# The first block's attention by pairs of heads instead of by tiles of tokens, in a fused attention and two-layer expert kernel

## The chip, the core and the metric

The kernel runs on one core of one Trainium2 chip. The metric is the device time of one launch in microseconds (us). The core has five engines with an instruction queue each: TensorE (PE, matmuls and transposes into PSUM), VectorE (DVE), ScalarE (ACT), GpSimd (POOL) and SyncE (SP, which issues the loads). They run independently and wait for each other by semaphores; each works through its own queue in order.

## What is computed

Linear attention with a normalisation, then a dense feed-forward layer with squared ReLU, then a feed-forward layer of 8 experts of which each token uses one. All inputs are float32.

```python
kv = np.einsum('bhsd,bhse->bhde', k, v)            # batch 4, heads 8, 576 tokens, head width 64
out = np.einsum('bhsd,bhde->bhse', q, kv)
rms = np.sqrt(np.mean(out * out, axis=-1, keepdims=True) + 1e-06)
x = out / rms * g_norm                             # then reshaped to 2304 tokens x 512
h = x @ w_in                                       # 512 -> 2048
x = np.maximum(h, 0.0) ** 2 @ w_out                # 2048 -> 512
logits = x @ w_gate                                # 8 experts; the largest one takes the token
y = gate * (np.maximum(x @ w1[e], 0.0) @ w2[e])    # e: the token's expert, within its capacity
```

## The kernel before

The 2304 tokens are 18 tiles of 128, in 6 blocks of TB = 3 tiles (BT = 384 tokens); a batch has 576 tokens, so block 0 lies inside batch 0. The 8 heads are 4 pairs of 128 columns.

**Attention of a block.** `kv(b, p)` multiplies k and v of pair p of batch b over five chunks into one PSUM bank (line 209) and copies the two 64 x 64 diagonal pieces into `kvb` (lines 211 and 212, ACT and DVE). `attn_out(t)` multiplies tile t of q with all four pairs of `kvb` (line 227), squares the result (line 235, ACT), sums the squares of each head (line 237, DVE) and takes mean and inverse root by a power (lines 239 and 241, POOL). `attn_mul(t)` scales the rows (line 245, DVE). `attn_tr(t)` transposes the four 128-column pieces (line 254, PE) and writes them as two float32r parts: the rounded value times `g_norm` (line 258, ACT) and the remainder (line 259, DVE). `xT[j]` of a block then holds [part, pair, token].

**First feed-forward layer.** Its hidden width 2048 is cut into NF = 16 slices f. A unit (j, f) is block j with slice f: `mm1` has 12 matmuls, three passes over each of the four 128-row chunks of `xT` (chunk c is pair c of the heads), then ReLU, square and split (lines 273 to 285), and `mm2`, two units later, adds its product to the block's output (line 292). Block 0 runs alone for LEAD = 4 units and then alternates with block 1. The tasks of block 1's attention are dealt out over units 0 to 3 by a plan.

**Weights of that layer.** They come in as 64-bit words (`load_m`, line 148). `cvt_m(f)` rebuilds float32 from the words: ACT scales the high halves of both matrices (line 167), DVE shifts and joins (lines 168, 169 and 173, on 1024 columns where both matrices go together). `split_m(f)` makes the float32r pair: a cast (line 182, ACT) and the remainder (line 183, POOL).

**Order.** `tc.manual_schedule(engines={SP})` (line 529) keeps the order of the code on SP's queue alone; on the other engines a scheduler orders the instructions. The loads come in the order pair 0 of k and v, two constants, pairs 1 to 3, the three q tiles, then words of f = 0 and f = 1, then the second batch's k and v with the words of f = 2 among them.

```python
        for p in range(NPAIR):
            kv(0, p)
        for t in range(TB):
            attn_out(t)
        for t in range(TB):
            attn_mul(t)
            attn_tr(t)
        for f in range(2):
            cvt_m(f)
            split_m(f, wpool)
```

Of the kernel before, what the change touches and what calls it, by code (L numbers as in the profile page):

```python
# [7 lines left out]
F32 = mybir.dt.float32  # L8
# [18 lines left out]
def attn_moe_kernel(ctx: ExitStack, tc: tile.TileContext, cap, kp, vp, qt, gn, wm, wg, wgt, w1, w2, ident, tri, out):  # L27
# [83 lines left out]
    def after_scatters(dma):  # L111
        dma = getattr(dma, "ins", dma)
        for i in scattered["disp"]:
# [27 lines left out]
    def load_m(f):  # L141
        for i in range(2):
            if f < 12:
                s = wpool.tile([P, 512], I64, tag="w", name="st64")
            else:
                s = stage.tile([P, 512], I64, tag="st", name="st64")
            stg["m", f, i] = s
            nc.sync.dma_start(out=s, in_=wm[f, :, i])

    def cvt_m(f):  # L150


        ws = [stg.pop(("m", f, i)).bitcast(I32).rearrange("p (n t) -> p n t", t=2) for i in range(2)]
        if f < 12:
            h = wpool2.tile([P, 2, 512], F32, tag="w", name="ch")
            o = wpool2.tile([P, 2, 512], F32, tag="w", name="cf")
            parts = [(h, o, slice(0, 2))]
# [6 lines left out]
        for h, o, sl in parts:  # L164
            hi, oi = h.bitcast(I32), o.bitcast(I32)
            for n, w in enumerate(ws[sl]):
                nc.scalar.activation(out=h[:, n, :], in_=w[:, :, 1].bitcast(F32), func=AF.Copy, scale=2.0 ** -112)
            nc.vector.tensor_scalar(oi, hi, -(1 << 31), None, op0=ALU.bitwise_and)
            nc.vector.scalar_tensor_tensor(
                out=oi, in0=hi, scalar=3, in1=oi, op0=ALU.logical_shift_left, op1=ALU.bitwise_or  # L170
            )
            for n, w in enumerate(ws[sl]):
                nc.vector.scalar_tensor_tensor(
                    out=oi[:, n, :], in0=w[:, :, 0], scalar=29, in1=oi[:, n, :],
                    op0=ALU.logical_shift_right, op1=ALU.bitwise_or,
                )

    def split_m(f, pool):
        os = cvt.pop(f)
        for o, d in zip(os, (wi, wo)):  # L180
            w = d[f] = pool.tile([P, 2, 512], F32R, tag="w", name="w")
            nc.scalar.copy(w[:, 0, :], o)  # L182
# [22 lines left out]
    def kv(b, p):  # L205
        k, v = kt.pop((b, p)), vt.pop((b, p))
        ps = misc()
        for c in range(NCH):
            nc.tensor.matmul(ps[:, :P], lhsT=k[:, c, :], rhs=v[:, c, :], start=c == 0, stop=c == NCH - 1)
# [52 lines left out]
        )  # L262


    gt = {}

    def mm1(s):
# [2 lines left out]
        n = 0  # L270
        for c in range(KD):
            for a, m in PASSES:
                nc.tensor.matmul(  # L273
                    h, lhsT=wi[f][:, a, c * P:(c + 1) * P], rhs=xT[j][:, m, c, :],
                    start=n == 0, stop=n == 3 * KD - 1,
                )
                n += 1


        r = gpool.tile([P, BT], F32, tag="rr", name="rr", bufs=2)  # L280
# [245 lines left out]
    MIDDLE = 416  # L526
    units = []

    with tc.manual_schedule(engines={mybir.EngineType.SP}):

        cold = gpool.tile([P, BT], F32, tag="rr", name="cold", bufs=2)[:, :P]
        nc.vector.memset(cold, 0.0)
# [10 lines left out]
        nc.vector.tensor_copy(ecap, ecap_i)  # L543
        nc.vector.tensor_copy(base, ecap_i)

        for p in range(NPAIR):
            load_kv(0, p)
            if p == 0:
                nc.sync.dma_start(out=id_sb, in_=ident)
                nc.sync.dma_start(out=gn_sb, in_=gn)  # L550
        for t in range(TB):
            load_q(t)
        load_m(0)
        load_m(1)
        load_kv(1, 0)
        load_kv(1, 1)
# [119 lines left out]
        for s in range(len(units)):  # L676
# [388 lines left out]
```

## Time and profile before

| what | value |
|---|---|
| median of 3 runs | 759.33 us (758.04 to 760.86) |
| the profiled execution's own time | 763.88 us |
| its span, first to last instruction | 762.10 us |
| busy: PE, DVE, ACT, POOL | 715.9, 370.7, 310.2, 292.1 us |
| mean granted clock of PE | 0.985 of full |
| 8.69 to 31.16 us: PE busy, DVE busy | 16.03, 13.63 of 22.47 us |
| 31.16 to 75.45 us: PE busy, DVE busy | 36.84, 40.41 of 44.29 us |
| 75.45 to 155 us: PE busy, DVE busy | 79.55, 51.00 of 79.55 us |

Times in the trace count from the first instruction of the span. A busy time is the union of an engine's instructions. Matmuls of float32 show as two records each (so the five matmuls of one `kv` are ten records), those of float32r as one. [...] "Idle before" an instruction is the time in which its engine had nothing to run, with the engine and line whose result ended it. DMA share 1.0 means that the core's 16 DMA engines were all moving data.

### The profile page before, as it was taken

Reading aid. Unit: us, or ns where it says so; the run is one execution under the profiler, and the core shown is the slowest. Engines: PE = TensorE matmul, PEld = TensorE weight load, DVE = VectorE, ACT = ScalarE, POOL = GpSimd, SP = SyncE. Lnnn points to the kernel's source line nnn. Section 1 sums busy time; section 2 is a strip of 40 time slices with the busy share of each in tenths; the row PEclk is TensorE's granted clock in tenths of the full one; section 3 lists DMA queues with packets and bytes.
Section 4 is the critical chain, followed back from the end, with each engine's and each line's share of the span. In section 5 each row is a group of like instructions: output and inputs, shape, how many; then the busy total and the mean of one; then the engine's idle time right before and its main releaser. Section 6 shows DMA issues by size and latency. Waiting matters only on the chain. (4 is left out here: it accounts for less than half of the span.)

```text
span 762.1 us, 11995 instructions
## 1 busy us (share of the span) xinstructions
PE 715.9 (94%) x3988; PEld 639.7 (84%) x3988; DVE 370.7 (49%) x829; ACT 310.2 (41%) x650; POOL 292.1 (38%) x288
## 2 busy tenths in 40 slices
PE   6688999999999999999999999999998999999874
PEld 6677999998999999889898988897887997898663
DVE  2989767448963593349445953331123220332011
ACT  2455455233222322232233354344367452665352
POOL 1576243112022200220220286224488637596570
PEclk9899999999999999999999999999999999999979
DMA  8946898311032202200100365152456536356520
GB/s 326 372 166 208 270 359 304 117 25 55 9 114 76 66 18 69 82 16 1 55 15 1 129 208 176 35 173 92 148 172 232 189 117 200 119 190 203 185 73 10
DMA packets 38020, 102.42 MB, mean 134 GB/s; under 512 B 4451, under 2 KB 4707, under 8 KB 37920
## 3 DMA queue, kind: packets, MB, share of 16 engines
q1 hardware_dynamic: 34912, 91.99, 36.0%
q0 software_dynamic: 3008, 9.10, 3.2%
q8 instruction: 63, 1.03, 0.6%
q14 instruction: 37, 0.30, 0.1%
HBM read 77.78 MB, written 23.91 MB: 133 GB/s over the span
## 5 line engine op out<-in xcount | busy, mean ns | idle before, releaser
L273 PE MATMUL pk<-xT,w 128*128 128x384 f32 x1152 | 223.1, 341 | 7.2 <-POOL w L183 4.6
L292 PE MATMUL pk<-w,g 128*128 128x512 f32 x864 | 218.4, 394 | 2.5 <-ACT g L284 2.5
L273 PEld LDWEIGHTS pk<-xT,w 128*128 128x128 f32 x1152 | 201.5, 188 | 17.0 <-POOL w L183 5.8
L194 POOL TENSOR_TENSOR w<-st,w 128x512 fp32r<-128x512 f32 x128 | 161.7, 1300 | 88.2 <-ACT w L190 86.6
L292 PEld LDWEIGHTS pk<-w,g 128*128 128x128 f32 x864 | 160.2, 188 | 31.7 <-ACT g L284 3.1
L281 ACT ACTIVATE rr<-pk 128x384 f32<-128x384 f32 x96 | 47.1, 492 | 153.3 <-PE pk L273 153.1
L810 PE MATMUL hb<-x,w 128*128 128x256 f32 (+2 forms) x672 | 95.3, 301 | 2.5 <-issue 1.7
L810 PEld LDWEIGHTS hb<-x,w 128*128 128x128 f32 x672 | 92.8, 188 | 4.2 <-issue 2.1
L864 DVE SCALAR_TENSOR_TENSOR g<-hb,g 128x576 fp32r<-128x576 f32 (+3 forms) x72 | 40.7, 585 | 106.2 <-ACT g L863 106.1
L283 DVE TENSOR_TENSOR pk<-pk,rr 128x384 f32<-128x384 f32 x96 | 54.0, 563 | 74.4 <-ACT rr L281 73.6
L102 POOL DMA_INDIRECT disp<-y,sli x18 | 19.1, 1059 | 173.1 <-DVE sli L409 52.9
L354 DVE SCALAR_TENSOR_TENSOR junk<-y,wgb 128x512 f32<-128x512 f32 x120 | 78.0, 684 | 0.7 <-ACT y L312 0.6
L190 ACT CAST w<-st 128x512 fp32r<-128x512 f32 x128 | 71.5, 620 | 11.6 <-DMA st<-in_w 11.1
L284 ACT CAST g<-pk 128x384 fp32r<-128x384 f32 x96 | 46.0, 480 | 72.4 <-DVE pk L283 70.6
L285 DVE TENSOR_TENSOR g<-pk,g 128x384 fp32r<-128x384 f32 x96 | 53.3, 556 | 36.6 <-ACT g L284 35.9
L183 POOL TENSOR_TENSOR w<-cf,w 128x512 fp32r<-128x512 f32 x32 | 46.8, 1482 | 61.4 <-ACT w L182 56.9
L896 PE MATMUL hb<-w,g 128*128 128x512 f32 x264 | 64.1, 399 | 2.9 <-DVE g L864 2.6
L896 PEld LDWEIGHTS hb<-w,g 128*128 128x128 f32 x264 | 48.9, 188 | 14.8 <-DVE g L864 3.2
L863 ACT ACTIVATE g<-hb 128x576 fp32r (+3 forms) x72 | 35.2, 513 | 33.7 <-PE hb L810 31.9
L102 POOL DMA_INDIRECT out<-o,meta x22 | 21.3, 970 | 46.8 <-ACT o L904 18.4
L912 DVE SCALAR_TENSOR_TENSOR o<-bk,meta,o 64x512 f32<-64x512 f32 x3 | 2.3, 753 | 69.1 <-ACT o L911 50.6
L239 POOL TENSOR_SCALAR ms<-ss 128x8 f32<-128x8 f32 x18 | 4.6, 255 | 77.0 <-DVE ss L237 76.7
(134 smaller groups left out, 651.1 us busy)
## 6 DMA issues: line engine op xcount, KB each, us to landing
st<-in_w SPq DMA_DIRECT2D x64, 512.0 KB
st<-in_wm SPq DMA_DIRECT2D x32, 512.0 KB
disp<-zrow SPq DMA_DIRECT2D x9, 1028.0 KB
xr<-disp SPq DMA_DIRECT2D x32, 257.0 KB
k<-in_kp SPq DMA_DIRECT2D x16, 320.0 KB
v<-in_vp SPq DMA_DIRECT2D x16, 320.0 KB
q<-in_qt SPq DMA_DIRECT2D x18, 256.0 KB
out<-zrow SPq DMA_DIRECT2D x9, 512.0 KB
```

The costliest lines, as they stand in the source:

```text
L183: nc.gpsimd.tensor_tensor(w[:, 1, :], o, f32(w[:, 0, :]), op=ALU.subtract)
L190: nc.scalar.copy(w[:, 0, :], s[:, i, :])
L194: e.tensor_tensor(w[:, 1, :], s[:, i, :], f32(w[:, 0, :]), op=ALU.subtract)
L273: nc.tensor.matmul(h, lhsT=wi[f][:, a, c * P:(c + 1) * P], rhs=xT[j][:, m, c, :], start=n == 0, stop=n == 3 * KD - 1,)
L281: nc.scalar.activation(out=r, in_=h, func=AF.Relu)
L283: nc.vector.tensor_tensor(h, h, r, op=ALU.mult)
L284: nc.scalar.copy(g[:, 0, :], h)
L285: nc.vector.tensor_tensor(g[:, 1, :], h, f32(g[:, 0, :]), op=ALU.subtract)
L292: nc.tensor.matmul(ysets[j == 1][i], lhsT=g[:, a, i * P:(i + 1) * P], rhs=wo[f][:, m, :], start=f == 0 and n == 0, stop=f == NF - 1 and n ...
L354: nc.vector.scalar_tensor_tensor(out=junk, in0=yt[j * TB + i][:, :DM], scalar=1.0, in1=wgb[e // 2][:, e % 2, :], op0=ALU.mult, op1=ALU.mul ...
L810: nc.tensor.matmul(h, lhsT=w1_at(e, f // 2, a, c)[:, f % 2 * P:(f % 2 + 1) * P], rhs=x[:, m, c, o:o + w], start=k == 0, stop=k == 3 * KD - 1,)
L896: nc.tensor.matmul(ps[:k, :], lhsT=lhs(f, a), rhs=we2[e, f][:, b, :], start=n == 0, stop=n == len(passes) * NF2 - 1,)
```

## The change

It rewrites the start of the program, up to the weights of f = 1, and leaves the rest as it is.

- **Loads**: after pair 0 of k and v and the two constants come the three q tiles, then pairs 1 and 2, the first matrix's words of f = 0, pair 3, the second matrix's words of f = 0, and from there on the old order.
- **Attention of block 0**: three new functions work on one pair of heads and all three tiles at a time. `first_out(p)` multiplies each q tile with pair p into 384 columns of one bank and does the squares, sums and power on six head-and-tile columns; `first_mul(p)` scales; `first_tr(p)` transposes three pieces and writes chunk p of `xT[0]`. So four operations of 384 columns stand where three of 512 stood. The PSUM banks go round over six (`pk[2:8]`) instead of three.
- **Words of f = 0**: rebuilt one matrix at a time on 512 columns, the first between the sums of pair 2 and the scaling of pair 1, the second between pair 2's transposes and the scaling of pair 3.
- **Order**: `tc.manual_schedule()` now holds the written order on all engines up to there. After it, `in_order` adds edges for the scheduler alone (no semaphore): ACT's scalings for f = 1 come after the last transposed chunk (`marks["first"]`), those for f = 2 after the casts of f = 1 (`marks["split"]`), and the matmuls of the second batch's `kv` in units 0 to 3 after unit 0's last matmul (`marks["kv"]`).

```diff
-        for p in range(NPAIR):
-            load_kv(0, p)
-            if p == 0:
-                nc.sync.dma_start(out=id_sb, in_=ident)
-                nc.sync.dma_start(out=gn_sb, in_=gn)
+        load_kv(0, 0)
+        nc.sync.dma_start(out=id_sb, in_=ident)
+        nc.sync.dma_start(out=gn_sb, in_=gn)
         for t in range(TB):
             load_q(t)
-        load_m(0)
+        load_kv(0, 1)
+        load_kv(0, 2)
+        load_m(0, (0,))
+        load_kv(0, 3)
+        load_m(0, (1,))
         load_m(1)
...
-        for p in range(NPAIR):
-            kv(0, p)
+        free[:] = pk[2:8]
+        kv(0, 0)
+        first_out(0)
+        kv(0, 1)
+        first_out(1)
+        first_mul(0)
+        first_tr(0)
+        kv(0, 2)
+        first_out(2)
+        c_in, c_out = cvt_m(0)
+        c_in()
+        first_mul(1)
+        first_tr(1)
+        split_m(0, wpool, (0,))
+        kv(0, 3)
+        first_out(3)
+        first_mul(2)
+        first_tr(2)
+        c_out()
+        first_mul(3)
+        first_tr(3)
+        split_m(0, wpool, (1,))
         for t in range(TB):
-            attn_out(t)
-        for t in range(TB):
-            attn_mul(t)
-            attn_tr(t)
-        for f in range(2):
-            cvt_m(f)
-            split_m(f, wpool)
+            qtt.pop(t)
+        free[:] = ysets[1]
+
+    with tc.manual_schedule(engines={mybir.EngineType.SP}):
+        marks["cvt"] = marks["first"]
+        for c in cvt_m(1):
+            c()
+        split_m(1, wpool)
+        marks["cvt"] = marks["split"]
```

The new functions:

```python
    def first_out(p):
        ps = ops[p] = misc()
        for t in range(TB):
            nc.tensor.matmul(
                ps[:, t * P:(t + 1) * P], lhsT=qtt[t][:, p, :], rhs=kvb[0][:, p, :],
                start=t == 0, stop=t == TB - 1, skip_group_check=True,
            )
        x = xst[p] = ypool.tile([P, ROW], F32, tag="y", name="x")[:, :BT] if p < 3 else apool.tile(
            [P, DM], F32, tag="x", name="x")[:, :BT]
        nc.scalar.activation(out=x, in_=ps[:, :BT], func=AF.Square)
        ss = small.tile([P, 2 * TB], F32, tag="ss", name="ss")
        nc.vector.tensor_reduce(out=ss, in_=x.rearrange("p (h e) -> p h e", e=DH), axis=AX.X, op=ALU.add)
...

    def first_mul(p):
        r, ps = rst.pop(p), ops.pop(p)
        nc.vector.tensor_tensor(
            xst[p].rearrange("p (h e) -> p h e", e=DH), ps[:, :BT].rearrange("p (h e) -> p h e", e=DH),
            r.rearrange("p (h o) -> p h o", o=1).to_broadcast([P, 2 * TB, DH]), op=ALU.mult,
        )

    def first_tr(p):
        x = xst.pop(p)
        ps = misc()
        for t in range(TB):
            nc.tensor.transpose(ps[:, t * P:(t + 1) * P], x[:, t * P:(t + 1) * P], id_sb)
        d = xt_tile(0)
        marks["first"] = nc.scalar.activation(out=d[:, 0, p, :], in_=ps[:, :BT], func=AF.Copy, scale=gn_sb)
        nc.vector.scalar_tensor_tensor(
            out=d[:, 1, p, :], in0=ps[:, :BT], scalar=gn_sb, in1=f32(d[:, 0, p, :]), op0=ALU.mult, op1=ALU.subtract,
        )
```

The order on PE, from the first `kv` on (`k`, `v`, `q`: loaded tiles; `kvb`: the products of pairs; `id_sb`: transposes; `pk`: PSUM banks; `xT,w`: `mm1`). Before:

```order
L209 MATMUL pk_92<-v,k 128x128 x5
L209 MATMUL pk_93<-v,k 128x128 x5
L209 MATMUL pk_94<-v,k 128x128 x5
L209 MATMUL pk_92<-v,k 128x128 x5
L227 MATMUL pk_93<-kvb_127,q 128x128 x4
L227 MATMUL pk_94<-kvb_127,q 128x128 x4
L227 MATMUL pk_92<-kvb_127,q 128x128 x4
L254 MATMUL pk_93<-id_sb,x 128x128 x4
L254 MATMUL pk_94<-id_sb,x 128x128 x4
L254 MATMUL pk_92<-id_sb,x 128x128 x4
L209 MATMUL pk_93<-v,k 128x128 x5
```

After, from the second pair on:

```order
L223 MATMUL pk_91<-v,k 128x128 x5
L285 MATMUL pk_92<-kvb_127,q 128x128 x3
L310 MATMUL pk_93<-id_sb,x 128x128 x3
L223 MATMUL pk_94<-v,k 128x128 x5
L285 MATMUL pk_89<-kvb_127,q 128x128 x3
L310 MATMUL pk_90<-id_sb,x 128x128 x3
L223 MATMUL pk_91<-v,k 128x128 x5
L326 MATMUL pk_87<-xT,w 128x384
L285 MATMUL pk_92<-kvb_127,q 128x128 x3
L326 MATMUL pk_87<-xT,w 128x384 x5
L310 MATMUL pk_93<-id_sb,x 128x128 x3
L326 MATMUL pk_87<-xT,w 128x384 x3
```

The four `kv` and three outputs that followed each other directly are now separated by the transposes of the pair before, and unit 0's matmuls stand among them; the second batch's `kv` (last row of the first piece) has moved behind unit 0.

The order on DVE over the same place (`ss`: sums of squares; `cf`, `ch`: rebuilt words; `st`: loaded words). Before, from the first sum on:

```order
L237 TENSOR_REDUCE ss<-x 128x8 x2
L245 TENSOR_TENSOR x<-pk_93,r 128x512
L237 TENSOR_REDUCE ss<-x 128x8
L245 TENSOR_TENSOR x<-pk_94,r 128x512
L168 TENSOR_SCALAR cf<-ch 128x1024
L259 SCALAR_TENSOR_TENSOR xT<-pk_93,gn_sb,xT 128x4x128
L259 SCALAR_TENSOR_TENSOR xT<-pk_94,gn_sb,xT 128x4x128
L245 TENSOR_TENSOR x<-pk_92,r 128x512
L169 SCALAR_TENSOR_TENSOR cf<-ch,cf 128x1024
L168 TENSOR_SCALAR cf<-ch 128x1024
```

After, from pair 2 on:

```order
L228 COPY kvb_127<-pk_94 64x64
L293 TENSOR_REDUCE ss<-x 128x6
L182 TENSOR_SCALAR cf<-ch 128x512
L183 SCALAR_TENSOR_TENSOR cf<-ch,cf 128x512
L187 SCALAR_TENSOR_TENSOR cf<-st_171,cf 128x512
L301 TENSOR_TENSOR x<-pk_92,r 128x384
L313 SCALAR_TENSOR_TENSOR xT<-pk_90,gn_sb,xT 128x384
L228 COPY kvb_127<-pk_91 64x64
L293 TENSOR_REDUCE ss<-x 128x6
L301 TENSOR_TENSOR x<-pk_89,r 128x384
L313 SCALAR_TENSOR_TENSOR xT<-pk_93,gn_sb,xT 128x384
```

The three operations on f = 0's first words stand ahead of the scaling of pair 1, and the words of f = 1, which before stood among the tiles, come only after the last chunk.

## Rows read from the trace of the kernel before

**Rows 1.** The page, first part: busy time, share of the span, instructions.
```profile
span 762.1 us, 11995 instructions
PE 715.9 (94%) x3988; PEld 639.7 (84%) x3988; DVE 370.7 (49%) x829; ACT 310.2 (41%) x650; POOL 292.1 (38%) x288
```

**Rows 2.** Busy time by stretch; the first line names the columns.
```profile
core 0: us, PE busy (x) PEld busy (x) DVE busy (x) ACT busy (x) POOL busy (x), PEclk, DMA share, GB/s
8.69:31.16 22.47, 16.03 (x103) 15.21 (x103) 13.63 (x23) 8.92 (x20) 6.53 (x9) 0.78 1.04 399
31.16:75.45 44.29, 36.84 (x199) 31.59 (x199) 40.41 (x51) 25.60 (x49) 32.21 (x22) 1.00 0.61 209
75.45:155.00 79.55, 79.55 (x400) 72.04 (x399) 51.00 (x79) 35.22 (x70) 22.32 (x19) 1.00 0.74 254
```

**Rows 3.** The same view, cut where the granted clock changes; columns as above.
```profile
8.30:11.70 3.40, 2.98 (x14) 3.01 (x15) 0.23 (x1) 0.21 (x1) 0.00 (x0) 0.50 1.03 405
11.70:21.90 10.20, 6.11 (x50) 5.42 (x49) 4.80 (x9) 4.17 (x9) 5.29 (x8) 1.00 1.04 407
21.90:28.70 6.80, 4.77 (x23) 4.80 (x24) 6.27 (x9) 2.50 (x5) 1.24 (x2) 0.50 1.04 384
```

**Rows 4.** PE's timeline, 0 to 37 us: start, length, what, [idle before, releaser].
```profile
4.96 1.28 PE L209 MATMUL pk<-v,k 128*128 128x128 f32 x10
8.72 5.00 PE L209 MATMUL pk<-v,k 128*128 128x128 f32 x30 [2.48 <-DMA v<-in_vp]
13.55 3.00 PE L227 MATMUL pk<-kvb,q 128*128 128x128 f32 x24
19.04 0.63 PE L254 MATMUL pk<-id_sb,x 128*128 128x128 f32 x4 [2.49 <-DVE x L245]
...
32.62 2.38 PE L273 MATMUL pk<-xT,w 128*128 128x384 f32 x12 [0.62 <-POOL w L183]
36.53 0.80 PE L273 MATMUL pk<-xT,w 128*128 128x384 f32 x3 [1.53 <-POOL w L183]
```

**Rows 5.** The timeline of all engines, DVE's rows, 18 to 31 us.
```profile
18.20 0.69 DVE L245 TENSOR_TENSOR x<-pk,r 128x512 f32<-128x512 f32 x1 [1.19 <-POOL r L241]
25.77 0.75 DVE L259 SCALAR_TENSOR_TENSOR xT<-pk,gn_sb,xT 128x512 fp32r<-128x512 f32 x1 [0.25 <-ACT xT L258]
29.15 1.29 DVE L173 SCALAR_TENSOR_TENSOR cf<-st,cf 128x512 int32<-128x512 int32 x2
```

**Rows 6.** Groups by line, 8 to 31.16 us: xcount | busy us, mean ns | idle before.
```profile
L169 DVE SCALAR_TENSOR_TENSOR cf<-ch,cf 128x1024 int32<-128x1024 int32 x2 | 2.4, 1218 | 0.0
L173 DVE SCALAR_TENSOR_TENSOR cf<-st,cf 128x512 int32<-128x512 int32 x4 | 2.6, 686 | 0.0
L245 DVE TENSOR_TENSOR x<-pk,r 128x512 f32<-128x512 f32 x3 | 2.1, 688 | 1.9 <-POOL r L241 1.9
L212 DVE COPY kvb<-pk 64x64 f32<-64x64 f32 x5 | 1.1, 228 | 6.5 <-ACT kvb L211 6.4
L254 PE MATMUL pk<-id_sb,x 128*128 128x128 f32 x12 | 2.3, 329 | 6.1 <-DVE x L245 6.1
L241 POOL TENSOR_TENSOR r<-ms,expo 128x8 f32<-128x8 f32 x3 | 5.2, 1739 | 0.2
L167 ACT ACTIVATE ch<-st 128x512 f32<-128x512 f32 x6 | 3.7, 664 | 0.0
L211 ACT COPY kvb<-pk 64x64 f32<-64x64 f32 x6 | 1.2, 204 | 10.0 <-PE pk L209 10.0
```

**Rows 7.** Groups by line, 75.45 to 155 us: the units' 384-column and the 512-column operations.
```profile
L283 DVE TENSOR_TENSOR pk<-pk,rr 128x384 f32<-128x384 f32 x20 | 11.3, 563 | 20.1 <-ACT rr L281 20.1
L168 DVE TENSOR_SCALAR cf<-ch 128x512 int32<-128x512 int32 x8 | 3.7, 468 | 0.0
L281 ACT ACTIVATE rr<-pk 128x384 f32<-128x384 f32 x20 | 9.8, 492 | 25.5 <-PE pk L273 25.4
```

**Rows 8.** Groups by line, 31.16 to 75.45 us: POOL's remainders and ACT's casts.
```profile
L183 POOL TENSOR_TENSOR w<-cf,w 128x512 fp32r<-128x512 f32 x16 | 25.4, 1612 | 19.3 <-ACT w L182 19.2
L182 ACT CAST w<-cf 128x512 fp32r<-128x512 f32 x15 | 8.9, 621 | 3.9 <-DVE cf L173 3.8
```

More of the change, by code (lines that the diff above doesn't have):

```diff
@@ L117, in after_scatters, with in_order @@
             )
+    def in_order(later, first):
+        later, first = getattr(later, "ins", later), getattr(first, "ins", first)
+        tc.add_manual_dep(
+            later, first.name, mybir.DependencyInfo(mybir.DependencyClass.NoSync, mybir.DependencyReason.SCHED_ONLY),
+            reason="the order in which the loads come in",
+        )
+    marks = {}
     kt, vt, qtt = {}, {}, {}
@@ L139, in load_w, with load_m @@
         nc.sync.dma_start(out=stg[key], in_=src)
-    def load_m(f):
-        for i in range(2):
+    def load_m(f, which=(0, 1)):
+        for i in which:
             if f < 12:
@@ L156, in cvt_m @@
             o = wpool2.tile([P, 2, 512], F32, tag="w", name="cf")
-            parts = [(h, o, slice(0, 2))]
+            parts = [(h[:, a:a + n], o[:, a:a + n], slice(a, a + n)) for a, n in (((0, 1), (1, 1)) if f == 0 else ((0, 2),))]
             cvt[f] = [o[:, i, :] for i in range(2)]
@@ L163, in cvt_m, with cvt_part, split_m @@
             cvt[f] = [o[:, 0, :] for o in os]
[L164 to L168, printed above, removed]
+        return [lambda part=part: cvt_part(ws, *part) for part in parts]
+    def cvt_part(ws, h, o, sl):
+        hi, oi = h.bitcast(I32), o.bitcast(I32)
+        for n, w in enumerate(ws[sl]):
+            a = nc.scalar.activation(out=h[:, n, :], in_=w[:, :, 1].bitcast(F32), func=AF.Copy, scale=2.0 ** -112)
+            if "cvt" in marks:
+                in_order(a, marks["cvt"])
+        nc.vector.tensor_scalar(oi, hi, -(1 << 31), None, op0=ALU.bitwise_and)
+        nc.vector.scalar_tensor_tensor(
+            out=oi, in0=hi, scalar=3, in1=oi, op0=ALU.logical_shift_left, op1=ALU.bitwise_or
+        )
+        for n, w in enumerate(ws[sl]):
             nc.vector.scalar_tensor_tensor(
-                out=oi, in0=hi, scalar=3, in1=oi, op0=ALU.logical_shift_left, op1=ALU.bitwise_or
-            )
[L172 to L182, printed above, removed]
+                out=oi[:, n, :], in0=w[:, :, 0], scalar=29, in1=oi[:, n, :],
+                op0=ALU.logical_shift_right, op1=ALU.bitwise_or,
+            )
+    def split_m(f, pool, which=(0, 1)):
+        for i in which:
+            o = cvt[f][i]
+            w = (wi, wo)[i][f] = pool.tile([P, 2, 512], F32R, tag="w", name="w")
+            marks["split"] = nc.scalar.copy(w[:, 0, :], o)
             nc.gpsimd.tensor_tensor(w[:, 1, :], o, f32(w[:, 0, :]), op=ALU.subtract)
@@ L208, in kv @@
         for c in range(NCH):
-            nc.tensor.matmul(ps[:, :P], lhsT=k[:, c, :], rhs=v[:, c, :], start=c == 0, stop=c == NCH - 1)
+            a = nc.tensor.matmul(ps[:, :P], lhsT=k[:, c, :], rhs=v[:, c, :], start=c == 0, stop=c == NCH - 1)
+            if "kv" in marks:
+                in_order(a, marks["kv"])
         d = kvb[b % 2]
@@ L272, in mm1 @@
             for a, m in PASSES:
-                nc.tensor.matmul(
+                a = nc.tensor.matmul(
                     h, lhsT=wi[f][:, a, c * P:(c + 1) * P], rhs=xT[j][:, m, c, :],
@@ L277, in mm1 @@
                 n += 1
+        if s == 0:
+            marks["kv"] = a
         r = gpool.tile([P, BT], F32, tag="rr", name="rr", bufs=2)
@@ L527, in attn_moe_kernel @@
     units = []
-    with tc.manual_schedule(engines={mybir.EngineType.SP}):
+    with tc.manual_schedule():
         cold = gpool.tile([P, BT], F32, tag="rr", name="cold", bufs=2)[:, :P]
@@ L683, in attn_moe_kernel @@
             if j == 0 and f + 2 < NF:
-                cvt_m(f + 2)
+                for c in cvt_m(f + 2):
+                    c()
+                marks.pop("cvt", None)
                 split_m(f + 2, wpool if f + 2 < 12 else wpool2)
@@ L694, in attn_moe_kernel @@
                 p_()
+            if s == LEAD:
+                marks.pop("kv", None)
             fl = s - at[NB - 1, 0]
```

13 lines of the change are left out of this document (added).

## The prediction

> **What bounds the kernel now.** The page's first part comes first [rows 1]: TensorE (PE) is busy 94% of a span of 762.10 us. The share of busy time in three stretches says where the rest is [rows 2]: from 75.45 us to 155 PE is busy without a gap, and in the two stretches before that it isn't. So a change that touches only the start is worth what it does to the moment at which that dense stretch begins, and the order of instructions shows that nothing after the first dozen feed-forward units moves. I therefore keep a ledger for PE from 8.69 us, where the second pair's matmuls begin, to the dense stretch: its matmuls are the same before and after, so the stretch begins later by whatever is added in idle time and in time lost at half clock.
>
> Before, the ledger reads: idle 22.47 - 16.03 = 6.44 us and then 44.29 - 36.84 = 7.45 us [rows 2]. [...] Sum 17.8 us.
>
> PE's timeline says what the idle time waits for [rows 4]: the second pair of k and v until 8.72 us, then the transposes for the normalised rows (6.1 us, released by VectorE (DVE) [rows 6]), then POOL's remainders of the weights for units 0 and 1. In the second stretch DVE is busy 40.41 of 44.29 us [rows 2]: it rebuilds weight words there. By 30.44 us (29.15 + 1.29) DVE has rebuilt the words of f = 0 and f = 1, and the last attention row leaves it at 26.52 us (25.77 + 0.75) [rows 5].
>
> **The change, part by part.** *Loads.* Three q loads (3 x 256 KB) go ahead of pairs 1 to 3. At 399 GB/s with the DMA engines full [rows 2] that is 1.9 us, so the second pair's matmuls start at 8.7 + 1.9 = 10.6 us. The q are then there by 9.0 us (640 KB earlier), so pair 0's output matmuls (0.75 us) run in that gap. The weight words fall between the pairs; bytes and number of loads are the same, f = 0's first half arrives near 13.5 us and is wanted near 19, so that part costs nothing.
>
> *A round.* PE now runs kv(p+1), output(p+1), transposes(p), and DVE reduce(p+1), multiply(p), remainder(p); each step waits for the one before on another engine. Durations: kv 1.28 (10 records); copies 0.20 on ScalarE (ACT) and 0.23 on DVE; output 12 matmuls in 3.00, so 0.75 for 3; transposes 0.63 for four, so 0.5 for three [rows 4, 6]. Operations of 384 columns do not stand there for attention; the nearest rows are the units' own, 0.49 on ACT and 0.56 on DVE [rows 7]; bounds are three quarters of the 512-column row (0.69, so 0.52) and that row itself [rows 6]. With 0.15 us from DVE to PE (18.20 + 0.69 to 19.04) and 0.03 elsewhere:
> 1.28 + 0.20 + 0.23 + 0.75 + 0.49 + 0.56 + 0.56 + 0.50 + about 0.5 of handovers = 5.1 us.
>
> Three such rounds make 15.2 us. POOL's power (1.74 [rows 6]) lies beside the next pair's steps. Before, the four kv ran back to back and the three tiles overlapped; now PE waits in every round.
>
> *Half of f = 0's words in the second round, half after the third.* DVE's three operations on 512 columns take 0.47 + 0.69 + 0.69 = 1.85 us [rows 6, 7], and they stand ahead of multiply(1) and multiply(3) in DVE's order, so both lie on the path: 1.95 us in round two; in the tail ACT 0.55 (transposed, between 0.49 and 0.69), 0.66 (words), DVE 1.85, multiply 0.56, transposes 0.65, ACT 0.55, DVE 0.56 and handovers, 5.5 us. The last remainder thus leaves DVE at 10.6 + 15.2 + 1.95 + 5.5 = 33.25 us, against 26.52: 6.7 us later at full clock. Unit 0, interleaved, ends 0.5 us behind it, near 33.8, against 34.6 before (ten matmuls from 32.62): that is what the change wins.
>
> *f = 1 and f = 2.* Their ACT scalings must now follow the last transposed chunk and f = 1's splits. After ACT's cast (0.62) and two scalings (1.33), DVE needs 0.69 + 1.22 + 1.29 and 1.13 for unit 0: f = 1 ends near 39.0 instead of 30.44, its first remainder near 41.2 (0.62 + 1.61 [rows 8]), and unit 1's third matmul, which began at 36.53 [rows 4], goes there. Behind it on PE wait unit 1, then attention tiles 3 to 5 and the next units. The 15 matmuls of three of the second block's kv pairs, now ordered behind unit 0, cost nothing: they fill PE's wait from 33.8 on.
>
> *Extra work.* Four operations where three stood: 4 x 0.56 - 3 x 0.69 = 0.17 us for each of reduce, multiply and remainder, 0.5 us of DVE in all, already in the walk. POOL's extra power (1.74) and the small operation ahead of it cost nothing: POOL is busy 6.53 of 22.47 us in that stretch [rows 2, 6].
>
> [...] In [rows 2] DVE is busy 13.63 of 22.47 us in the first stretch, while PE waits 6.1 us for it. [...]
>
> *Sum.* PE's work between 8.69 and 33.8 us: 0.75 + 3 x 1.28 + 3 x 0.75 + 4 x 0.5 + 2.38 (unit 0's twelve [rows 4]) = 11.2 us, idle 25.1 - 11.2 = 13.9. For the rest I take the idle time of before, 7.45 less the 0.62 inside unit 0 [rows 4], 6.8 us: DVE and POOL have the same list there. It could be 3.9 less, DVE's whole idle time in that stretch, or 2 more, since f = 1 and f = 2 now come one after the other. At full clock: 13.9 + 6.8 - 17.8 = +2.9 us. Half clock: before, it followed PE's gap of 6.24 to 8.72, then 16.55 to 21.9, where PE ran 1.26 us. The first gap stays, so most of kv(1) runs at half (0.9 lost); if the path's PE steps (3.84 + 2.25 + 2.0 and 0.4 of unit 0, 8.5 us) get it for the same share as before (7.75 of 16.03), 4.1 is lost. I take the middle, 2.5. Sum **+5.4 us**: 759.33 + 5.4 = **764.7**. The ledger is that of the profiled execution, which took 763.88 us (span 762.10), 4.55 above the median; a profiled one after the change would be near 763.88 + 5.4 = 769.3. The 384-column steps at their bounds move the walk by -0.4 to +1.3 us (some ten of them on the path).
>
> **Rivals.** *Overlap wins (not slower).* If the spread-out matmuls keep the clock at full (0 lost) and DVE has no idle time behind 33.8: 2.9 - 3.9 = -1.0, 758.3; if besides the rounds hide the weight words (1.95 + 1.85 = 3.8 us), -4.8, 754.5. For it: DVE is only 61% busy in the first stretch. Against: in DVE's order the words stand ahead of multiply. It decides if the last remainder leaves DVE before about 29 us. [...]
> *DVE's backlog absorbs it.* If DVE closes up its 3.88 us of idle time [rows 2] and the clock costs 0.9: 2.9 + 0.9 - 3.9 = -0.1, 759.2. For: DVE is the busiest there; against: its waits are chains through POOL and PE that stay.
> *Half clock throughout.* PE idles 13.9 of 25.1 us in the new walk against 6.44 of 22.47; were the clock at half for all of the path, 8.5 instead of 2.5: 2.9 + 8.5 = +11.4, 770.7 at most; with half of the added 6.0 hidden, +8.4, 767.7. For: both earlier drops followed sparse stretches; against: PE's gap from 16.55 to 19.04 us did not end the full clock until 21.9 [rows 3, 4]. [...]
>
> **Chances.** Forecast (+3 to +8) 0.55, half clock throughout 0.15, absorbed 0.2, overlap wins 0.1. About 0.5%, 3.8 us, is what a measurement here can tell from no change. Four fifths of the first case and the second lie beyond it (0.44 + 0.15, less 0.01 for the walk's own error): slower 0.58; faster than 755.5 only with the words hidden too, 0.07; same 0.35. The range takes the absorbed end with the clock's lower bound and reaches to the half-clock case: 759.0 to 768.5.
>
> **What would show it.** Right: second kv near 10.6 us; transposes at intervals of 5 us or more; the last remainder (a 384-column write of xT on DVE) near 33 us or later; unit 0 done near 34 and unit 1's third matmul past 40; dense stretch later by 3 to 8 us. Wrong: that remainder before 29 us, or unit 1 before 37. If those times come late and the dense stretch isn't later, the idle time behind 33.8 us was mis-sized.

## The result, and the profile after

The changed kernel takes 770.89 us (median of 4, 770.39 to 771.19), the kernel before 760.1 (758.04 to 764.13): ratio 1.0136, interval 1.0108 to 1.0164. It is 10.8 us slower where the forecast had 5.4 more, and outside the range. The direction was forecast, and so were both mechanisms, waits in every round and half clock; the size of the second wasn't.

The profiled execution took 770.39 us. The page's first part [rows 1 before]:

```profile
span 768.6 us, 12006 instructions
PE 724.1 (94%) x3988; PEld 644.7 (84%) x3988; DVE 368.1 (48%) x834; ACT 310.3 (40%) x652; POOL 290.3 (38%) x290
```

PE does the same 3988 matmuls in 8.2 us more busy time, so the clock is the first suspect. PEclk is the share of full speed that the profile shows as granted to PE; "full clock" is a PEclk of 1.00, "half clock" one of 0.50. Busy time by stretch, cut where it changes; the last row is the same 31 us that are used below to compare kernels:

```profile
core 0: us, PE busy (x) PEld busy (x) DVE busy (x) ACT busy (x) POOL busy (x), PEclk, DMA share, GB/s
10.50:31.00 20.50, 13.76 (x58) 12.18 (x57) 5.95 (x12) 4.25 (x10) 6.92 (x9) 0.50 0.99 377
31.00:34.40 3.40, 1.90 (x9) 1.09 (x8) 2.02 (x4) 1.19 (x3) 1.52 (x2) 1.00 0.57 186
34.40:41.20 6.80, 4.68 (x17) 3.40 (x17) 4.11 (x8) 2.71 (x5) 1.27 (x1) 0.50 0.21 78
41.20:68.50 27.30, 22.57 (x134) 18.78 (x133) 21.20 (x33) 15.10 (x31) 15.67 (x13) 1.00 0.51 174
68.50:71.90 3.40, 2.86 (x11) 2.69 (x12) 1.61 (x3) 0.69 (x1) 2.17 (x2) 0.50 0.00 0
8.69:40.00 31.31, 19.54 (x76) 15.77 (x76) 11.43 (x22) 8.42 (x18) 10.12 (x13) 0.58 0.82 307
```

The same 31 us of the kernel before:

```profile
8.69:40.00 31.31, 22.72 (x141) 21.38 (x142) 21.36 (x31) 13.98 (x30) 15.34 (x15) 0.84 0.99 380
```

Against [rows 3]: half clock for 20.5 us at a stretch, through the first three of the attention's four pairs, then twice more, with PE busy 13.76 + 4.68 + 2.86 = 21.3 us instead of 7.75. DVE, which was busy 21.36 of these 31.31 us, is now busy 11.43.

PE's timeline [rows 4 before], the serial rounds and unit 1:

```profile
10.20 2.25 PE L223 MATMUL pk<-v,k 128*128 128x128 f32 x10 [1.40 <-DMA v<-in_vp]
13.01 1.65 PE L285 MATMUL pk<-kvb,q 128*128 128x128 f32 x6 [0.56 <-DVE kvb L228]
16.41 0.90 PE L310 MATMUL pk<-id_sb,x 128*128 128x128 f32 x3 [1.76 <-DVE x L301]
17.11 2.34 PE L223 MATMUL pk<-v,k 128*128 128x128 f32 x10
...
25.29 0.90 PE L310 MATMUL pk<-id_sb,x 128*128 128x128 f32 x3 [3.63 <-DVE x L301]
...
38.02 1.66 PE L326 MATMUL pk<-xT,w 128*128 128x384 f32 x3 [0.67 <-ACT xT L312]
...
46.01 1.32 PE L326 MATMUL pk<-xT,w 128*128 128x384 f32 x6 [0.23 <-POOL w L197]
```

The reader should see both things at once: each round waits in series as forecast (kv, output, transposes, each behind another engine), and each PE step in it is far longer than at full clock: kv 2.34 us where 1.28 stood, output 1.65 (0.75 was expected, and it took 0.94 with the clock at 1.00, as shown below). On DVE [rows 5 before], the reductions of pairs 1 to 3, the last remainder and the end of f = 1's words:

```profile
15.21 0.55 DVE L293 TENSOR_REDUCE ss<-x 128x6 f32<-128x384 f32 x1 [2.26 <-ACT x L291]
22.21 0.55 DVE L293 TENSOR_REDUCE ss<-x 128x6 f32<-128x384 f32 x1 [2.26 <-ACT x L291]
31.09 0.55 DVE L293 TENSOR_REDUCE ss<-x 128x6 f32<-128x384 f32 x1 [2.26 <-ACT x L291]
38.00 0.62 DVE L313 SCALAR_TENSOR_TENSOR xT<-pk,gn_sb,xT 128x384 fp32r<-128x384 f32 x1 [1.61 <-ACT xT L312]
42.72 1.28 DVE L187 SCALAR_TENSOR_TENSOR cf<-st,cf 128x512 int32<-128x512 int32 x2
```

Rounds of 7.0 and 8.9 us, the last remainder done at 38.6.

**The gauge.** Unit 24 lies well inside the dense stretch of every kernel, behind all that was edited. Its row in PE's timeline, the kernel before, then the change:

```profile
142.49 2.24 PE L273 MATMUL pk<-xT,w 128*128 128x384 f32 x12
```

```profile
152.91 2.24 PE L326 MATMUL pk<-xT,w 128*128 128x384 f32 x12
```

The 10.4 us were already there at unit 8 (75.45 and 85.87) and stay the same from there to unit 24, so the whole loss arises before the dense stretch. From unit 24 to the end the profiled executions of all kernels below take 611 to 620 us, in no relation to where unit 24 begins; so mechanisms are judged by unit 24's start, and times with their intervals stand beside it. Unit 24's start is read from one profiled execution of each kernel.

### The profile page after: what moved, and what is told of

The parts are those of the page before. It is cut to its first block, busy times and chain, and to the rows that moved or that the text cites. A ratio compares the mean times of both kernels' runs of the same rounds, so it can differ in the third digit from the quotient of the medians.

```text
span 768.6 us, 12006 instructions
## 1 busy us (share of the span) xinstructions
PE 724.1 (94%) x3988; PEld 644.7 (84%) x3988; DVE 368.1 (48%) x834; ACT 310.3 (40%) x652; POOL 290.3 (38%) x290
## 5 line engine op out<-in xcount | busy, mean ns | idle before, releaser
L326 PE MATMUL pk<-xT,w 128*128 128x384 f32 x1152 | 227.1, 343 | 7.6 <-POOL w L197 3.7
L197 POOL TENSOR_TENSOR w<-cf,w 128x512 fp32r<-128x512 f32 x32 | 44.9, 1418 | 68.8 <-ACT w L196 68.7
L102 POOL DMA_INDIRECT out<-o,meta x22 | 21.3, 969 | 45.0 <-ACT o L987 18.4
L979 PE MATMUL bk<-w,g 128*128 128x512 f32 x120 | 28.6, 396 | 0.0
```

Of the source, the lines that this page charges most:

```text
L326: a = nc.tensor.matmul(h, lhsT=wi[f][:, a, c * P:(c + 1) * P], rhs=xT[j][:, m, c, :], start=n == 0, stop=n == 3 * KD - 1,)
L979: nc.tensor.matmul(ps[:k, :], lhsT=lhs(f, a), rhs=we2[e, f][:, b, :], start=n == 0, stop=n == len(passes) * NF2 - 1,)
```

## Experiments

Three theories. **Clock**: the waits inside the serial rounds keep TensorE at half clock, and that is most of the 10.4 us. **Chain**: the hops through ACT, DVE and POOL are the loss, whatever the clock. **Backlog**: DVE's and POOL's list of weight words, put later by the ordering marks, decides. Each ratio in the table is to runs of the kernel before that were made beside it, so ratios can be compared from row to row and medians less well.

| kernel | unit 24 at, us | against 142.49 | median, us | ratio to before (interval) |
|---|---|---|---|---|
| the change | 152.91 | +10.42 | 770.89 | 1.0136 (1.0108 to 1.0164) |
| all waits filled | 146.07 | +3.58 | 764.79 | 1.0067 (1.0031 to 1.0103) |
| only the wait for pair 1 filled | 152.29 | +9.80 | 770.59 | 1.0139 (1.0089 to 1.0188) |
| only the rounds filled | 146.20 | +3.71 | 761.14 | 1.0011 (0.9983 to 1.0039) |
| without the marks | 157.43 | +14.94 | 776.35 | 1.0205 (1.0171 to 1.0239) |
| f = 0's words behind | 150.16 | +7.67 | 769.14 | 1.0110 (1.0069 to 1.0151) |
| words behind, waits filled | 146.30 | +3.81 | 759.48 | 0.9980 (0.9959 to 1.0002) |
| before, waits filled | 142.55 | +0.06 | 758.25 | 0.9949 (0.9921 to 0.9978) |
| loads alone | 146.67 | +4.18 | 765.45 | 1.0071 (1.0044 to 1.0098) |
| loads alone, waits filled | 147.65 | +5.16 | 762.37 | 1.0009 (0.9987 to 1.0031) |
| overlapped pairs, waits filled | 138.93 | -3.56 | 755.58 | 0.9912 (0.9883 to 0.9940) |
| overlapped pairs | 141.43 | -1.06 | 759.68 | 1.0003 (0.9976 to 1.0030) |

**All waits filled.**

```diff
+        def fill(n):
+            for i in range(n):
+                nc.tensor.matmul(pk[1][:, :P], lhsT=cold, rhs=cold, start=True, stop=True)
         kv(0, 0)
+        fill(1)
         first_out(0)
+        fill(7)
         kv(0, 1)
+        fill(1)
         first_out(1)
+        fill(5)
...
         first_tr(2)
+        fill(9)
```

Expected: 

> The changed kernel with 38 idle matmuls (128 columns, on a zeroed tile, into a bank that nobody reads) put into TensorE's waits of the four rounds; nothing else is moved. Clock theory: what the rounds cost beyond the forecast is TensorE at half clock (busy 21.3 us of it up to the dense stretch, against 7.75 before), and that comes from the waits inside the rounds. Then the granted clock stays at full from about 7 us on, the last remainder of xT leaves DVE near 34 instead of 38.6, unit 8 begins at 78 to 81 instead of 85.9, and the time is 763 to 766. Chain theory: the hops through ACT, DVE and POOL make the time and TensorE's own steps are a small part; then the clock is full as well, but the last remainder stays past 37, unit 8 at 84 to 86, the time 768 to 771. Backlog theory: the rounds end early as in the clock theory, but DVE's and POOL's list of weight words decides the units after them, and unit 8 stays past 83 (767 or more).

Measured: unit 24 at 146.07, 6.84 us earlier than with the change. Busy time by stretch (columns as above), then PE's (unit 24 last) and DVE's timelines:

```profile
8.69:40.00 31.31, 24.98 (x184) 22.10 (x183) 15.88 (x31) 11.44 (x25) 12.33 (x15) 1.00 0.92 341
```

```profile
15.28 1.28 PE L223 MATMUL pk<-v,k 128*128 128x128 f32 x10
17.11 0.94 PE L285 MATMUL pk<-kvb,q 128*128 128x128 f32 x6 [0.33 <-DVE kvb L228]
17.89 2.17 PE L594 MATMUL pk<-cold 128*128 128x128 f32 x18
21.70 0.55 PE L310 MATMUL pk<-id_sb,x 128*128 128x128 f32 x3 [1.64 <-DVE x L301]
...
39.15 2.03 PE L326 MATMUL pk<-xT,w 128*128 128x384 f32 x10 [0.52 <-POOL w L197]
...
146.07 2.24 PE L326 MATMUL pk<-xT,w 128*128 128x384 f32 x12
```

```profile
13.69 0.55 DVE L293 TENSOR_REDUCE ss<-x 128x6 f32<-128x384 f32 x1 [1.55 <-ACT x L291]
18.61 0.55 DVE L293 TENSOR_REDUCE ss<-x 128x6 f32<-128x384 f32 x1 [1.55 <-ACT x L291]
25.42 0.55 DVE L293 TENSOR_REDUCE ss<-x 128x6 f32<-128x384 f32 x1 [1.55 <-ACT x L291]
31.98 0.62 DVE L313 SCALAR_TENSOR_TENSOR xT<-pk,gn_sb,xT 128x384 fp32r<-128x384 f32 x1 [1.25 <-ACT xT L312]
```

(Each idle matmul leaves two records, so x18 are nine.) PE executes more matmuls than with the change alone and is done earlier: the clock is granted at full (1.00 instead of 0.58) from 8.69 to 40 us, kv takes 1.28 us, the rounds 4.9 and 6.8 us, and the last remainder is done at 32.6 instead of 38.6. The clock theory holds: 6.84 of 10.42 us are clock. The chain theory's 84 to 86 us for unit 8 is out (79.03); the 3.58 us that are left could be its part.

**Which waits bring the half clock?** Two runs with one part of the idle matmuls each.

```diff
         kv(0, 0)
+        fill(1)
         first_out(0)
+        fill(7)
         kv(0, 1)
```

Expected: 

> The changed kernel with eight idle matmuls only ahead of pair 1 (one before pair 0's outputs, seven in the wait for the second k and v); the waits inside the rounds stay. Unit 24 began at 142.5 before, 152.9 after the change and 146.1 with all waits filled. If the wait for the loads is what brings the half clock, the clock is full through the rounds and unit 24 begins at 146 to 147. If the rounds by themselves are too sparse (clock theory as the forecast's third rival has it), the clock falls within the first two rounds and unit 24 begins at 149 to 152.

Expected of the counterpart, which has all the others: 

> The counterpart: 30 idle matmuls inside the rounds, none ahead of pair 1. If the rounds are what keeps the clock down, it is at half for pair 1's steps only (from about 10.5 us, some 3 to 5 us of TensorE's work, 1 to 2 us lost), then full, and unit 24 begins at 147 to 148.5. If the wait for the loads decides, the clock stays at half through the rounds in spite of the idle matmuls (which are then twice as long and come in the way), and unit 24 begins at 152 or later.

Busy time by stretch of the first, then of the second:

```profile
8.69:15.20 6.51, 4.19 (x33) 3.66 (x32) 1.89 (x4) 1.19 (x3) 2.25 (x4) 0.97 1.03 407
15.20:38.00 22.80, 14.77 (x60) 11.80 (x60) 9.66 (x18) 7.38 (x15) 7.89 (x10) 0.65 0.81 310
```

```profile
8.69:15.20 6.51, 4.24 (x32) 3.67 (x33) 1.89 (x4) 1.19 (x3) 2.24 (x4) 1.00 1.03 406
15.20:38.00 22.80, 18.84 (x141) 16.71 (x140) 13.44 (x25) 9.23 (x21) 7.98 (x11) 1.00 0.92 339
```

With only the wait for the loads filled, the granted clock is 0.97 from 8.69 to 15.2 us, where pair 1 runs, and 0.65 from there to 38 us, where the waits in the rounds are left open: unit 24 at 152.29, nothing gained to speak of (just past the far end of what was expected). With only the rounds filled it is at 146.20, as with all of them. The second expectation was too careful: in that execution not even pair 1 ran at half clock (1.00 from 8.69 to 15.2 us), though the wait for the loads stayed open. So in these two runs the half clock went with the waits inside the rounds (0.65 with them open, 1.00 with them filled), not with the wait for the loads in front of them.

**The ordering marks.**

```diff
-        marks["cvt"] = marks["first"]
         for c in cvt_m(1):
             c()
         split_m(1, wpool)
-        marks["cvt"] = marks["split"]
```

Expected: 

> The changed kernel without the two ordering marks that keep the words of f = 1 and f = 2 behind the attention (the order of instructions then has both ahead of pair 1's remainder on DVE, some 6.5 us of work). Backlog theory (the marks make the loss, DVE rebuilds f = 1 and f = 2 too late): unit 1 follows unit 0 at once and unit 8 begins at 80 to 83, the time 765 to 768. Clock and chain theories (the rounds make it, the marks protect them): the last remainder goes from 38.6 to 44 or later, unit 0's end with it, unit 8 is no earlier than 85.9 and up to 90, the time 771 to 775.

DVE's timeline:

```profile
25.41 0.68 DVE L182 TENSOR_SCALAR cf<-ch 128x1024 int32<-128x1024 int32 x1
...
33.09 1.29 DVE L187 SCALAR_TENSOR_TENSOR cf<-st,cf 128x512 int32<-128x512 int32 x2
34.42 0.23 DVE L228 COPY kvb<-pk 64x64 f32<-64x64 f32 x1
...
43.83 0.62 DVE L313 SCALAR_TENSOR_TENSOR xT<-pk,gn_sb,xT 128x384 fp32r<-128x384 f32 x1 [1.61 <-ACT xT L312]
```

From 25.4 to 34.4 us DVE does little but rebuild the words of f = 1 and f = 2, and pair 3's copy comes behind them; the last remainder is done at 44.45. Unit 24 comes 4.5 us later than with the marks (776.35 us, a little past the 771 to 775 expected). The marks don't cause the loss, they limit it.

**f = 0's words out of the chain**, at half clock and with the waits filled.

```diff
-        c_in()
         first_mul(1)
         first_tr(1)
+        c_in()
...
-        c_out()
         first_mul(3)
         first_tr(3)
+        c_out()
```

Expected: 

> The changed kernel with the words of f = 0 out of the chain: the first half's three DVE operations behind pair 1's remainder instead of ahead of pair 1's multiply, the second half's behind the last remainder. Chain theory: both stood on the path (1.95 + 1.85 us in the forecast), so the last remainder leaves DVE near 34.8 instead of 38.6 and unit 8 begins 3 to 4 us earlier, near 82.3; time 767. Clock theory: the same 3.8 us at the rounds, and the rest of the loss (7 us) stays, because the clock stays at half; unit 8 at 82 to 83. Backlog theory: the words only change places in DVE's list, so unit 8 stays at 85 to 86, 770 to 771.

Expected with the waits filled as well: 

> The changed kernel with idle matmuls in TensorE's waits and f = 0's words behind the multiplies at once. Alone they brought unit 8 from 85.9 to 79.0 and to 82.7. If clock and chain are separate terms, they add: 79.0 - 3.2 = 75.8, the clock full from about 7 us, the time 761 to 762, the kernel before within half a per cent. If DVE's and POOL's list of words holds the later units once the rounds are short (backlog theory), unit 8 stays at 78 to 79, 764.

At half clock the last remainder is done at 35.7 instead of 38.6, unit 8 begins at 82.65, 3.2 us earlier and about where it was expected, and unit 24 is 2.75 us earlier. Not all of that need be the words: the granted clock from 8.69 to 40 us was 0.64 instead of 0.58, and pair 3's output ran at full clock (0.94 us).

With the waits filled the same move gains nothing (unit 24 at 146.30 against 146.07, unit 8 at 78.76). But the edit took only half of the words out of the chain. On ACT the cast of the first words (line 196), which waits for DVE to rebuild them, still stands ahead of the copy of pair 3's kv (line 227). ACT's timeline of the run with the waits filled:

```profile
23.84 0.62 ACT L196 CAST w<-cf 128x512 fp32r<-128x512 f32 x1 [1.94 <-DVE cf L187]
24.37 0.20 ACT L227 COPY kvb<-pk 64x64 f32<-64x64 f32 x1
```

Pair 3's kv was done at 21.83, so its copy began 2.5 us late, and DVE's reductions of pairs 2 and 3 are 7.4 us apart there against 6.8 without the move. The clock wasn't quite held either (0.94, with 27 idle matmuls instead of 38). So this run doesn't settle whether clock and chain add. The second half's words did leave the rounds, and unit 1 still begins at 38.03 us with the move and 37.86 without: f = 1's words stand on DVE behind the attention and behind f = 0's, in whichever order these two come. For that half the backlog theory is right. The median of 759.48 us is lower than unit 24 makes it; that difference wasn't pursued.

**The kernel before with its waits filled.** The ledger charged it 3.9 us of half clock, half of the 7.75 us (2.98 + 4.77) that PE was busy at a clock of 0.50 [rows 3]; was that worth anything?

```diff
         for p in range(NPAIR):
             kv(0, p)
+            if p == 0:
+                fill(8)
         for t in range(TB):
             attn_out(t)
+        fill(8, kvb[0][:, NPAIR - 1, :])
         for t in range(TB):
             attn_mul(t)
             attn_tr(t)
+            if t < 2:
+                fill(3, kvb[0][:, NPAIR - 1, :])
```

Expected: 

> The kernel before with 22 idle matmuls: eight in the wait for the second pair, eight ahead of the first transposes, three behind each of two. Clock theory, with the forecast's ledger: its half clock (busy 7.75 us, 3.9 lost) goes, and unit 8 begins at 71.5 to 73 instead of 75.45, the time 756 to 758. Backlog theory: DVE is busy 40.41 of 44.29 us behind 31.16 and its list hides what TensorE loses; the clock is full, and unit 8 stays at 75 to 75.5, 759 to 761. (Some of the idle matmuls may come in the way of the transposes, a quarter of a us at a time.)

```profile
8.69:31.16 22.47, 17.13 (x131) 15.30 (x131) 14.20 (x22) 10.28 (x22) 9.22 (x11) 1.00 1.04 398
31.16:75.45 44.29, 35.55 (x192) 30.34 (x191) 40.51 (x52) 24.43 (x47) 30.04 (x21) 1.00 0.61 209
```

The half clock is gone (1.00 instead of 0.78 [rows 2] from 8.69 to 31.16 us) and unit 1 begins 2.1 us earlier (32.36 against 34.48), but unit 2 begins at 39.23 against 39.43, unit 3 at 47.03 against 46.95, and unit 24 at 142.55: nothing is left of it. DVE is busy 40.51 of 44.29 us as before, and its words hold unit 2, on PE's timeline and on DVE's:

```profile
39.23 2.39 PE L273 MATMUL pk<-xT,w 128*128 128x384 f32 x12 [2.22 <-DVE g L285]
```

```profile
34.94 2.27 DVE L173 SCALAR_TENSOR_TENSOR cf<-st,cf 128x512 int32<-128x512 int32 x2
```

The words of f = 2 end at 37.21 (37.03 in the kernel before), and only behind them does DVE come to the units' own operations. The clock theory's ledger failed here: what the kernel before lost on PE did not hold the units behind it. The run is also a control: the 22 idle matmuls with the clock at full moved unit 24 by 0.06 us. The ratio, 0.9949, can't come from there; in the profiled executions the difference lies behind unit 24 (616.0 us against 619.6).

**The loads alone**, in the kernel before, by its tiles.

```diff
-        for p in range(NPAIR):
-            load_kv(0, p)
...
-        load_m(0)
+        load_kv(0, 0)
+        nc.sync.dma_start(out=id_sb, in_=ident)
+        nc.sync.dma_start(out=gn_sb, in_=gn)
+        for t in range(TB):
+            load_q(t)
+        load_kv(0, 1)
+        load_kv(0, 2)
+        load_m(0, (0,))
+        load_kv(0, 3)
+        load_m(0, (1,))
```

Expected: 

> The kernel before with the loads' new order and nothing else (tile by tile, three q ahead of pairs 1 to 3, the first weight words between pairs). The forecast's price for the loads is 1.9 us for all that hangs on the second pair, the walk then goes on as before: unit 8 near 77.4 against 75.45, time 761 to 762. If the loads cost more than that by the clock (the longer gap ahead of the second pair brings the half clock on earlier and for longer), unit 8 comes at 79 or later, time 764 or more; if the other waits hide them, it stays at 75.5, 759.

Expected with the waits filled: 

> The kernel before with the loads' new order and with the 22 idle matmuls that left its unit 24 at 142.5. Alone, the loads' order moved it to 146.7. If 1.9 us of that is the second pair's later arrival and the rest half clock, as the forecast has it, unit 24 begins at 144 to 145. If DVE's list decides there too (the words are ahead of the reductions in its order now), the idle matmuls change nothing: 146 to 147.

Both are inconclusive. By its numbers alone the first is the costlier case of the expectation (unit 8 at 78.79, 765.45 us, the clock 0.67 against 0.84 before). Pair 1's matmuls began at 10.49 us, as forecast, but the scheduler also arranged DVE's, ACT's and PE's work anew, with the first operation on f = 0's words ahead of the first reduction. In the second run the clock wasn't held either (0.76 from 8.69 to 40 us), and unit 24 came at 147.65, past both values expected. What the loads' order costs by itself stays open; the forecast's 1.9 us is neither shown nor refuted.

**Overlapped pairs.** Do the 3.58 us left at full clock come from the pairs or from the serial rounds? Here kv(p+2) goes ahead of pair p's transposes and output(p+2) right behind them, so that a pair's power on POOL runs beside other pairs' matmuls.

```diff
         first_out(1)
         first_mul(0)
-        first_tr(0)
         kv(0, 2)
+        first_tr(0)
         first_out(2)
-        c_in, c_out = cvt_m(0)
-        c_in()
         first_mul(1)
-        first_tr(1)
-        split_m(0, wpool, (0,))
         kv(0, 3)
+        c_in, c_out = cvt_m(0)
+        c_in()
+        first_tr(1)
         first_out(3)
+        split_m(0, wpool, (0,))
+        fill(6)
         first_mul(2)
         first_tr(2)
-        c_out()
+        fill(5)
         first_mul(3)
         first_tr(3)
+        c_out()
```

(Besides, the small tiles of the powers get a buffer per pair parity, and the wait for pair 1 is filled as above.)

Expected: 

> The changed kernel with the pairs overlapped: kv(p+1) ahead of the transposes of pair p - 1, multiply(p) behind kv(p+2)'s place, so that a round no longer waits for its own power on POOL; the second half of f = 0's words last; idle matmuls in the waits that are left. Chain theory (the serial rounds are the +2.9 of the forecast): the last remainder leaves DVE at 23 to 25 against 26.52 before and 38.6, unit 8 begins at 71 to 74, time 756 to 758. Backlog theory: the remainder is early as well, but the list of words holds unit 8 at 75 or later, 760 or more.

Expected without the idle matmuls: 

> The same overlapped pairs without the idle matmuls. Clock theory: TensorE waits less in the rounds, but the wait for the second pair stays (7.9 to 10.2 us), so the clock falls there and stays at half for part of the attention; the steps at half rate add 2 to 4 us to the run with idle matmuls, unit 8 at 74 to 77, time 758 to 762. If the clock doesn't matter once the pairs overlap, the two runs agree within 0.5 us at unit 8.

With them, busy time by stretch, DVE's last remainder and unit 24:

```profile
8.69:40.00 31.31, 26.41 (x186) 22.57 (x184) 21.70 (x39) 15.93 (x34) 13.64 (x17) 1.00 1.01 385
```

```profile
25.62 0.62 DVE L313 SCALAR_TENSOR_TENSOR xT<-pk,gn_sb,xT 128x384 fp32r<-128x384 f32 x1 [1.96 <-ACT xT L312]
```

```profile
138.93 2.24 PE L326 MATMUL pk<-xT,w 128*128 128x384 f32 x12
```

DVE is busy 21.70 us of the 31.31 instead of 11.43 (15.88 with serial rounds at full clock). The last remainder is done at 26.24, a little past what was expected, unit 24 begins 7.14 us earlier than with serial rounds at the same clock, and the kernel beats both: 755.58 us, ratio 0.9912 (0.9883 to 0.9940). This edit does two things: it overlaps the pairs, and it takes f = 0's words out of the chain, ACT's cast of the first ones included. The nearest run with serial rounds and the words behind, with waits filled, has its last remainder at 32.15, 5.9 us later, of which the late copy of pair 3 shown above is 2.5. By that estimate some 3.4 us of the 5.9 are the overlap; no run has it alone. Without idle matmuls the clock is 0.84 in the same stretch and unit 24 comes 2.5 us later, as the clock theory has it; no gain over the kernel before can be measured then.

## Why the prediction was wrong

- **Loads.** Second kv forecast at 10.6 us, began at 10.20: right.
- **The walk of the rounds.** Right, for the clock it was made for. With the clock held, DVE's reductions are 4.9 and 6.8 us apart (forecast 5.1 and 7.05), the last remainder is done at 32.6 (33.25), unit 0 at 33.3 (33.8), unit 1's third matmul at 39.15 (41.2). Of the parts of a round, the output was sized too short (0.94 us against 0.75), with the whole still right. In the changed kernel itself the same points came at 38.6, 39.7 and 46.0.
- **The sum at full clock.** Forecast +2.9, measured +3.58, with some luck: up to unit 8 PE, the idle matmuls left out, idles 18.1 us there (forecast 13.9 + 6.8 = 20.7), and its work takes 3.2 us more than the 49.0 that the ledger's estimate gives for the kernel before at full clock (52.87 - 3.9).
- **The step that failed** is the clock term: "I take the middle, 2.5". The measured value is 6.84 us, outside the 0.9 to 4.1 of which 2.5 is the middle; only the rival's 8.5 lay beyond it. In the ledger of the changed kernel itself 21.3 / 2 = 10.65 us are lost at half clock, by the estimate that half of PE's busy time at 0.50 is lost, and the idle time is 17.0 us (31.00 - 19.23 up to 39.69 us, 46.17 - 40.91 from there to unit 8) instead of 20.7: by that estimate part of what the clock lost lay in time that would have been idle. Here the clock stayed at half through the whole of the first three rounds (0.50 from 10.5 to 31.0 us). The rival "half clock throughout", given 0.15, comes closest to what happened: it said 767.7 to 770.7, and 770.89 was measured. Its argument on the other side, that one wait of 2.5 us hadn't ended the full clock before, looked at one wait; here they return in every round. The run with all waits filled agrees with this rival: 38 idle matmuls on a tile of zeros brought the clock of these 31 us from 0.58 to 1.00.
- **Where 2.5 came from.** The upper bound of 4.1 rested on the share that the kernel before had (7.75 of 16.03 us of PE's busy time), though the walk itself said that PE would idle 13.9 of 25.1 us. That share was also applied wrongly: it is one of time, not of work. By work (3.9 of 12.2 us lost) the same 8.5 us lose 2.7, and the sum would have come out lower still.
- **The 3.9 us of half clock** in the ledger's 17.8 for the kernel before (6.44 + 7.45 + 3.9) are the author's estimate, half of the 7.75 us that PE was busy at 0.50 [rows 3]. No run shows them as a loss: with the waits filled and the clock at 1.00, unit 24 moved by 0.06 us. Half clock there slowed work in front of a unit that DVE held anyway. In the changed kernel it slowed the very matmuls that DVE waits for. DVE's waits from 8.69 to 40 us (total us, times, longest), the change and then the run with all waits filled:

```profile
DVE ss L293 <- ACT x L291: 8.3, 4, 2.3
DVE xT L313 <- ACT xT L312: 6.1, 4, 1.6
DVE kvb L228 <- ACT kvb L227: 5.1, 3, 2.8
```

```profile
DVE ss L293 <- ACT x L291: 6.2, 4, 1.6
DVE xT L313 <- ACT xT L312: 5.0, 4, 1.3
DVE kvb L228 <- ACT kvb L227: 3.0, 1, 3.0
```

  ACT's reads of PE's results are what DVE waits for in all three rows; 5.3 of the 6.84 us are found there.
- **Words on the path.** f = 0's words did lie on the path to the last remainder as the walk had them: with the clock held, the round with the first half takes 6.8 us and the one without 4.9, 1.9 more (forecast 1.95). What they cost the dense stretch is less certain. Moving them gave 2.75 us at unit 24 at half clock, part of which may be the clock, against 3.8 in the sum. With the waits filled it gave nothing, but there the first half stayed on the path through ACT's cast; the second half only changed places with f = 1's, which the sum did not see.
- **f = 1 and f = 2.** They came late as forecast; that the marks which make them late are worth 4.5 us, because the scheduler would otherwise put both ahead of pair 3, wasn't.
- **The wait for DVE's multiply**, PE's 6.1 us before [rows 6], stayed. After the change that wait is 7.5 us (PE's waits, 8.69 to 40 us):

```profile
PE pk L310 <- DVE x L301: 7.5, 4, 3.6
```

  The shorter operations in this serial chain didn't let the work end sooner. Overlapped and with the waits filled, they did (ratio 0.9912); overlapped without idle matmuls, nothing could be measured (1.0003).

## What to carry to other kernels

Cutting this work into rounds with a wait on TensorE in each had two prices, the waits and the clock, and the second was the larger: 6.84 of the 10.42 us at unit 24 went when the clock was held at 1.00, and 3.58 stayed. So cost such a chain once more with every PE step at the length that it had here at half clock (kv 2.34 us for 1.28, output 1.65 for 0.94, transposes 0.90 for 0.55) before trusting the sum. A few idle matmuls in those waits told which of the two it was. Time at half clock counted here where the next engine in the chain waited for just those matmuls (5.3 of the 6.84 us are in DVE's waits); in the kernel before, where DVE held the next units (busy 40.41 of 44.29 us), removing it moved unit 24 by 0.06 us. And when work is moved out of a chain, follow it on every engine's queue: words that had left DVE's path still held up a copy on ACT, by 2.5 us.

## What was not expected of the hardware

- The clock stayed at half for 20.5 us at a stretch (10.5 to 31.0 us, PE busy 13.76 us of it), and 38 matmuls on a tile of zeros whose results nobody reads kept it at full over the same rounds (1.00 from 8.69 to 40 us).
- With only the wait for the loads filled, pair 1 ran at full clock and the rounds did not (0.97 from 8.69 to 15.2 us, 0.65 from there to 38): full clock at the beginning of these sparse rounds wasn't kept through them. (With only the rounds filled, pair 1 ran at full clock too, 1.00 from 8.69 to 15.2 us.)
- The part behind unit 24 differs by 8.3 us between the profiled executions of kernels that are alike there (611.3 to 619.6 us). From unit 24's start to that of unit 95, the last of the first feed-forward layer, it is 329.0 to 331.4 us in all of them, so nearly all of the difference lies in the 282 to 290 us behind unit 95's start. The granted clock is part of it at most: from 700 us to 9 us before the end it was 0.90 in the kernel before (619.6), but the mean of the whole profiled run, 0.985 there, was 0.994 with all waits filled (615.8) and 0.992 with the words behind as well (611.3). The rest stays open.
